# Block products in 13 of 16 half passes, sums in idle accumulator rows, early routing, and one chain for the last two passes

## The chip, the core and the metric

One core of a Trainium2 chip runs the whole program. The metric is device time in microseconds (us) of one execution, as a median of three timed runs: 757.85 us for the kernel before (757.56 to 758.64). Matrix products run on TensorE (PE, with PEld for its weight loads), elementwise work on VectorE (DVE), ScalarE (ACT) and GpSimd (POOL); SyncE (SP) issues nearly all transfers.

## The reference, cut to what matters

```
# 1. decayed linear attention, 2 x 8 heads, 768 tokens, head size 64  ->  x[1536, 512]
# 2. dense mixture, 4 experts, hidden 1024
for e in range(4):
    out += p[:, e:e+1] * (np.maximum(x @ w1[e], 0.0) @ w2[e])      # p: normalised domain_probs
# 3. mixture with one expert of 8 per token
logits = out @ w_gate;  expert_idx = argmax(logits);  gate_w = max(softmax(logits))
for e in range(8):
    mask = expert_idx == e
    y[mask] = gate_w[mask, None] * (np.maximum(out[mask] @ w1b[e], 0.0) @ w2b[e])
```

All in float32. The kernel writes each operand of a product as a high part (rounded to the fp32r type) and a low part (the remainder) and forms three products, high x high, low x high and high x low.

## The kernel before

**Passes.** Stage 2 is cut into 16 half passes `k` = 0 to 15. Passes 0 to 7 work on the first slab of 768 tokens, 8 to 15 on the second; `k % 8` names an expert and a half of its hidden units (512). A half pass multiplies `x` by a half of `w1` (the "h" products, with a relu and a split of the result) and then by a half of `w2` (the "y" products). Each y tile of 128 tokens is added into `acc[:, t, :]`, by DVE, or written there by ACT where `k % 8 == 0`.

**Plain and block passes.** A plain pass makes h with four row blocks and all tokens: 96 matmuls of 384 columns. A block pass (`fast_unit`, lines 567 to 631) splits `w1` and the tokens into 2 x 2 blocks and makes seven products in place of eight, as Strassen and Winograd do: 84 matmuls of 384 columns (`line` holds their order, product and half). It needs sums of weight blocks (`s1` to `s4`, made in `fast_steps`) and sums of token blocks (`t1` to `t4`), each as a high and a low part. Before, `FAST` holds 11 passes: 2 to 7 and 9 to 13. Passes 0, 1, 8, 14 and 15 are plain. During passes 1 and 8 (`plain_unit`) the token sums of the slab are made in small pieces (`tokens_steps`, lines 531 to 559), with scratch tiles of 384 columns.

**Kept weights.** The four tiles of weight blocks that a block pass of the first slab makes are stored to DRAM (`kept`) and fetched for the second slab's pass on the same expert half (`kept_steps`): passes 10 to 13 before.

**Attention** runs beside pass 0: `att_step` puts its matmuls between those of the pass, so many per unit as `paces` says. For the first slab its result goes straight into `xh` and `xl`, for the second into `x2`.

**Routing.** Each of 12 token tiles gets logits, a choice of expert (`route_choose`), a rank inside the expert and a scatter of its rows to DRAM rows `bins` (`route_send`). The logits of tiles 0 to 5 are made by DVE as row sums (`logit_v`, 8 per tile, one per expert, against rows of `wgt` in a ring of five buffers inside `x2`); those of tiles 6 to 11 by PE, with four transposes (`rtr`, `route_x`) and four small matmuls (`lg`). `bins` is first filled by one transfer (`open_routing`). Before, that fill and the routing of all tiles stand in passes 14 and 15, which run as three groups of 256 tokens, in each group pass 14 and then pass 15 (`moe1_group`).

**Order.** The program is recorded by hand in order (`manual_schedule`), and each engine runs its own instructions strictly in that order. `split_to(w, k, n)` makes the next `n` weight pieces as far as pass `k`; the hooks `hook1` (after each of 14 block products) and `hook2` (after each of 6 y tiles) place everything that isn't a matmul of the pass. PSUM gives three rotating banks `mm` to y tiles and plain h products, and four banks to the block products: product 1 of half `s` is copied by ACT to SBUF (`keep`, line 598) before products 6, 7 and 4 go on in its bank.

Of the kernel before, what the change touches and what calls it, by code (L numbers as in the profile page):

```python
# [40 lines left out]
FAST = [k for k in range(2, K1 - 2) if k != KS]  # L41
KEPT = [k for k in FAST if k >= KS and k - KS in FAST]
# [18 lines left out]
VT = TT  # L61
# [3 lines left out]
def body(ctx: ExitStack, tc: tile.TileContext, lam, att, dp, w1a, w2a, wg, wgt, w1b, w2b, out):  # L65
# [29 lines left out]
    lg_v = const.tile([P, TT, E2], F32, name="lg_v")  # L95
# [40 lines left out]
    def load_piece():  # L136
# [5 lines left out]
        if k < K1:  # L142
            src, e = (w1a, w2a)[w], k % KS // 2
        else:
            src, e = (w1b, w2b)[w], nth[(k - K1) // 2]
# [28 lines left out]
    def split_plain(n, c):  # L174
# [22 lines left out]
        k: dram.tile([len(PAIRS), P, 4, HF], F32, name=f"kept{k}") for k in FAST if k + KS in KEPT  # L197
# [7 lines left out]
    def fast_steps(n):  # L205
# [30 lines left out]
        def third():  # L236
            part("a22", raw(1, 1))
            add("s3", raw(0, 0), raw(0, 1), ALU.subtract)
            drop_raw()

        def fourth():
            add("s4", raw(1, 0), got["s2"], ALU.subtract, got["s2"])
            drop_raw()
            part("s1", got["s1"])

        return [
            sums,
            lambda: part("a11", raw(0, 0)),
            lambda: part("a12", raw(1, 0)),
            third,  # L250
            lambda: part("s2", got["s2"]),
            fourth,
            lambda: part("s3", got["s3"]),
            lambda: part("s4", got["s4"]),
        ]

    def kept_steps(n):
# [137 lines left out]
    def att_o(c):  # L395
# [29 lines left out]
        for r in range(2):  # L425
# [3 lines left out]
            else:  # L429
                hi_lo(xh[:, d, o:o + CH], xl[:, d, o:o + CH], xo[r], V)  # L430

# [63 lines left out]
    def moe1_mm2(k, hs, t0, j, midway=None, late="r"):  # L495
        t = t0 // P + j
        e = k % KS // 2
        ps = ps_mm.tile([P, 512], F32, tag="mm", name=f"y{k}_{t}")
        wh, wl = wt[1, k]
        parts = [((hh[:, j * P:j * P + P], hl[:, j * P:j * P + P]), (wh[:, f, :], wl[:, f, :]))  # L500
                 for f, (hh, hl) in enumerate(hs)]
        if midway:
            mm3(ps, parts[:FC // 2], True, False)
            midway()
            parts = parts[FC // 2:]
# [25 lines left out]
    def tokens_steps(g):  # L531
        def sums(d):
            f = {}

            def block(r, j):
                if g:
                    return x2[:, 2 * r + d, j * TH:j * TH + TH]
                return f[r, j]

            def whole():  # L540
                for i, (r, j) in enumerate([(0, 0), (0, 1), (1, 1), (1, 0)]):
                    f[r, j] = tmp(i, f"x{r}{j}_{d}")
                    a, b = (x[:, 2 * r + d, j * TH:j * TH + TH].bitcast(F32) for x in (xh, xl))
                    G.tensor_tensor(out=f[r, j], in0=a, in1=b, op=ALU.add)

            def one(n, i, a, b, op):
                t = f[n] = tmp(i, f"t{n}_{g}_{d}")
                V.tensor_tensor(out=t, in0=a(), in1=b(), op=op)  # L548
                hi, lo = st[f"t{n}"]
                hi_lo(hi[:, d, :], lo[:, d, :], t, V)  # L550

            return ([] if g else [whole, None]) + [
                lambda: one(1, 4, lambda: block(0, 1), lambda: block(0, 0), ALU.subtract),
                lambda: one(3, 5, lambda: block(1, 1), lambda: block(0, 1), ALU.subtract),
                lambda: one(2, 4, lambda: f[3], lambda: block(0, 0), ALU.add),
                lambda: one(4, 5, lambda: block(1, 0), lambda: f[2], ALU.subtract),
            ]

        return sums(0) + sums(1)

    def tokens_split(j):
        c = slice(j * TH, j * TH + TH)
        hi_lo(xh[:, :, c], xl[:, :, c], x2[:, :, c], V)


# [75 lines left out]
    def open_routing():  # L641
# [11 lines left out]
        for i in range(EN):  # L653
            G.memset(od["caps"][:, i:i + 1], float(BY_RANK[i]))
        rp = rt["rp"] = rt_ctx.enter_context(pool("rp", 2, side="right"))
        rt["ps_rt"] = rt_ctx.enter_context(pool("ps_rt", 2, space=PSUM))
        rt["ps_sm"] = rt_ctx.enter_context(pool("ps_sm", 3, space=PSUM))
# [5 lines left out]
        fill = rp.tile([P, W], F32, name="fill", bufs=1)  # L663
        G.memset(fill, 0.0)
        G.memset(fill.bitcast(I32)[:, DM + 1:W], FAR)
        SP.dma_start(
            out=bins.rearrange("(n p) w -> p n w", p=P),
            in_=fill.unsqueeze(1).to_broadcast([P, E2 * MOST // P, W]),
        )
# [29 lines left out]
    def route_choose(t, midway=None):  # L699
        rp = rt["rp"]  # L700
        if t < VT:
            lg = lg_v[:, t, :]
        else:
            xt = rt.pop((t, "xt"))
            lg = rt["ps_sm"].tile([P, P], F32, tag="sm", name=f"lg{t}")[:, :E2]
# [35 lines left out]
    def route_place(t):  # L741
        rp = rt["rp"]
# [4 lines left out]
        rank = rt["ps_sm"].tile([P, P], F32, tag="sm", name=f"rank{t}")[:, :E2]  # L747
# [20 lines left out]
    def route_row(t):  # L768
        gs = rt.pop((t, "gs"))
        pos = rt["rp"].tile([P, 1], I32, tag="pos", name=f"pos{t}", bufs=4)  # L770
# [55 lines left out]
    def route_order():  # L826
        count, place, places = od["count"], od["place"], od["places"]
        by_pair = od["tmp"][:, :EN * EN].rearrange("p (a b) -> p a b", a=EN)
        sm = rt["ps_sm"].tile([P, P], F32, tag="sm", name="counts")[:, :E2]
# [54 lines left out]
    def keep_up(n):  # L884
        warmup(rt["ps_sm"].tile([P, P], F32, tag="sm", name="warm_rt"), n)


    with tc.manual_schedule():
# [66 lines left out]
        def att_step():  # L955
# [8 lines left out]
            elif s == 1:  # L964
# [3 lines left out]
                if c == NC - 1:  # L968
                    at_ctx.close()
            else:  # L970
# [6 lines left out]

        rsteps = []
        rstage = (route_x, route_choose, lambda t: None, route_send)

        def route_step(t=None):

            for i, (t0, r) in enumerate(list(rsteps)):
                rstage[r](t0)
                rsteps[i] = (t0, r + 1)
            rsteps[:] = [x for x in rsteps if x[1] < len(rstage)]
            if t is not None:
                rsteps.append((t, 1 if t < VT else 0))

        paces = {0: (0, 1, 2, 2, 1, 0), 256: (1, 2, 2, 2, 1, 0), 512: (1, 2, 2, 2, 1, 0)}  # L990

        def moe1_group(k, t0, n, units, early=None):
            assert done["c"] >= (t0 + n) // CH - 1
            hs = []
            early = early or []

            def steps_of(i):
                for _ in range(paces[t0][i] if k == 0 and asteps else 0):
                    att_step()

            last = t0 + n == N
            for f in range(FC):
                hs.append(moe1_mm1(k, t0, n, f))
                steps_of(f)
                route_step(early.pop(0) if early else None)
                units(f)
            for j in range(n // P):
                t = t0 // P + j
                if t == NC - 1 and k == KL:
                    while rsteps:  # L1010
                        route_step()
                    first_load()
                    first_high(NC - 2)
                    split_to(0, k + 2, 2)
                    first_low(NC - 2)
                    moe1_mm2(k, hs, t0, j, lambda: route_x(NC - 2))
                    continue
                if last and k == KL:
                    split_to(0, k + 2, 2)
# [511 lines left out]
```

## Time and profile before

| | us |
|---|---|
| median of three timed runs | 757.85 |
| the profiled execution, its own time | 758.02 |
| span of its trace | 756.0 |
| pass 0 with attention (20.06 to 82.05) | 61.99 |
| pass 1, plain (82.05 to 116.88) | 34.83 |
| a block pass (148.45 to 179.99) | 31.54 |
| pass 8, plain (306.15 to 341.59) | 35.44 |
| passes 14 and 15, three groups | 24.11, 25.87, 27.41 |
| the rest, from 577.15 | 178.85 |

The profile shows one execution. An engine's busy time is read from its instructions; matmuls are pipelined, so a busy PE can still hide short stalls, and the time that a stretch takes is read from the starts in the chain of waits. That chain follows the work that ended last back to what released it.

### The profile page before, as it was taken

To read this page: it belongs to the slowest core of one execution; us is meant where nothing else is said; L and a number is where in the kernel's file an instruction comes from. 1 tells how busy PE (TensorE), PEld (TensorE's weight loads), DVE (VectorE), ACT (ScalarE), POOL (GpSimd) and SP (SyncE) were. 2 spreads that over 40 slices of the span, in tenths; PEclk is the share of its full clock that TensorE was granted. 3 is DMA by queue.
4 is the path that set the end of the run, shared out by engine and by line. 5 is a ranking of instruction groups with operands and counts; after the bars stand their busy time and mean duration, and the time that the engine had idled before them with its cause. 6 is when DMAs were issued, how large, how long until landed. Compare 5 with 4: busy or idle time off the path is not lost.

```text
span 756.0 us, 12472 instructions
## 1 busy us (share of the span) xinstructions
PE 740.2 (98%) x4736; PEld 667.5 (88%) x4736; DVE 494.4 (65%) x1079; ACT 309.6 (41%) x676; POOL 93.5 (12%) x98
## 2 busy tenths in 40 slices
PE   7999999999999999999999999999999999999995
PEld 7888889898898988889889898988898998998994
DVE  7444377676856767555377777777457867675883
ACT  4223335353343534345133141522124756665673
POOL 4563220000000000000000000003111013121013
PEclk9999999999999999999999999999999999999998
DMA  9774126627351122116171642286113877865660
GB/s 295 266 234 159 56 73 234 237 69 279 122 212 56 56 83 84 57 54 250 73 258 55 231 141 111 85 299 218 43 56 130 291 217 248 290 190 191 234 221 29
DMA packets 34314, 122.59 MB, mean 162 GB/s; under 512 B 4114, under 2 KB 6162, under 8 KB 31180
## 3 DMA queue, kind: packets, MB, share of 16 engines
q1 hardware_dynamic: 32139, 115.47, 44.6%
q0 software_dynamic: 2112, 6.31, 2.2%
q8 instruction: 38, 0.62, 0.3%
q14 instruction: 25, 0.20, 0.1%
HBM read 96.04 MB, written 25.92 MB: 161 GB/s over the span
## 4 chain that ended last, share of the span: by engine, by line
PE 73%; issue 17%; DVE 4%; POOL 2%; DMA 2%; ACT 1%; SPq 0%; POOLq 0%; ACTq 0%
PE y L469 35%; PE b L593 21%; PE h L469 9%; POOL out L112 2%; DMA att<-in_att 2%; PE qk L357 1%; PE xo L420 1%; PE xo L413 1%; PE z L1186 1%; DVE w1l L172 1%; PE lg L707 1%; PE u L441 0%; ACT w1h L171 0%; PE rtr L694 0%; DVE t L548 0%
## 5 line engine op out<-in xcount | busy, mean ns | idle before, releaser
L510 DVE SCALAR_TENSOR_TENSOR acc<-y,p_sb,acc 128x512 f32<-128x512 f32 x84 | 63.0, 750 | 65.3 <-PE y L469 62.1
L172 DVE TENSOR_TENSOR w1l<-raw,w1h 128x512 fp32r<-128x512 f32 x124 | 83.0, 692 | 16.6 <-ACT w1h L171 16.2
L171 ACT CAST w1h<-raw 128x512 fp32r<-128x512 f32 x128 | 75.3, 617 | 0.0
L600 ACT COPY u<-b 128x384 f32<-128x384 f32 x66 | 31.1, 475 | 100.2 <-PE b L593 98.9
L469 PE MATMUL h<-xh,w0h 128*128 128x256 f32 (+1 forms) x208 | 57.9, 308 | 1.0 <-ACT w0h L171 1.0
L172 DVE TENSOR_TENSOR w0l<-raw,w0h 128x512 fp32r<-128x512 f32 x80 | 52.5, 697 | 6.8 <-ACT w0h L171 6.3
L469 PE MATMUL h<-xh,w0l 128*128 128x256 f32 (+1 forms) x208 | 56.2, 298 | 0.0
L171 ACT CAST w0h<-raw 128x512 fp32r<-128x512 f32 x98 | 55.8, 619 | 0.3 <-DMA raw<-in_w1a 0.2
L593 PE MATMUL b<-xh,w0h 128*128 128x384 f32 x176 | 48.9, 338 | 0.0
L648 POOL IOTA places<- 128x7 f32 x1 | 0.2, 161 | 385.9 <-PE y L469 385.9
L112 POOL DMA_INDIRECT out<-y,xb x16 | 30.2, 1885 | 134.9 <-DVE y L1302 84.1
L469 PEld LDWEIGHTS h<-xh,w0h 128*128 128x128 f32 x208 | 38.2, 188 | 2.5 <-ACT w0h L171 1.2
L469 PEld LDWEIGHTS h<-xh,w0l 128*128 128x128 f32 x208 | 38.4, 189 | 0.4
L469 PE MATMUL g<-xg,w0h 128*128 128x288 f32 (+1 forms) x192 | 38.1, 293 | 0.0
L607 DVE TENSOR_TENSOR u<-b,u 128x384 f32<-128x384 f32 x66 | 36.4, 552 | 2.4 <-PE b L593 2.4
L469 PE MATMUL h<-xl,w0h 128*128 128x256 f32 (+1 forms) x208 | 37.0, 299 | 0.0
L684 DVE CUSTOM_DVE_ANT_0 x<-acc,x 128x512 f32<-128x512 f32 x48 | 32.9, 686 | 0.6
L593 PEld LDWEIGHTS b<-xh,w0h 128*128 128x128 f32 x176 | 32.3, 188 | 0.5
L469 PEld LDWEIGHTS h<-xl,w0h 128*128 128x128 f32 x208 | 31.2, 188 | 0.0
L469 PEld LDWEIGHTS g<-xg,w0h 128*128 128x128 f32 x192 | 30.8, 189 | 0.0
L593 PE MATMUL b<-xl,w0h 128*128 128x384 f32 x88 | 29.8, 339 | 0.0
L1186 PE MATMUL z<-g,w1h 128*128 128x352 f32 (+2 forms) x96 | 29.1, 366 | 0.8 <-DVE g L1208 0.7
(305 smaller groups left out, 2015.8 us busy)
## 6 DMA issues: line engine op xcount, KB each, us to landing
raw<-in_w2a SPq DMA_DIRECT2D x32, 512.0 KB, 3.6
raw<-in_w1b SPq DMA_DIRECT2D x32, 512.0 KB, 5.4
raw<-in_w2b SPq DMA_DIRECT2D x32, 512.0 KB, 4.9
att<-in_att SPq DMA_DIRECT2D x24, 512.0 KB, 5.1
raw<-in_w1a SPq DMA_DIRECT2D x22, 512.0 KB, 4.3
kept<-w0h SPq DMA_DIRECT2D x8, 1024.0 KB, 4.2
w0h<-kept SPq DMA_DIRECT2D x8, 1024.0 KB, 6.6
bins<-fill SPq DMA_DIRECT2D x1, 4626.0 KB
```

Of the source, the lines that this page charges most:

```text
L112: i = G.indirect_dma_start(out=dst, out_offset=bass.IndirectOffsetOnAxis(ap=idx, axis=0), in_=src, in_offset=None, bounds_check=rows - 1, ...
L171: A.copy(out=hi, in_=src)
L172: eng.tensor_tensor(out=lo, in0=src, in1=hi.bitcast(F32), op=ALU.subtract)
L357: T.matmul(qk[r][:, h, :], kT[64 * r:64 * r + 64, h, :], qT[64 * r:64 * r + 64, h, :], start=True, stop=True,)
L413: T.matmul(xo[r][o, h // 2, :], st[q, h, :], qd[q, h, :], start=h < 2, stop=False, skip_group_check=True,)
L469: T.matmul(ps, l, r, start=first and i == 0, stop=last and i == len(ops) - 1)
L510: V.scalar_tensor_tensor(out=acc[:, t, 0:DM], in0=ps, scalar=p_sb[:, t, e:e + 1], in1=acc[:, t, 0:DM], op0=ALU.mult, op1=ALU.add,)
L593: T.matmul(ps, l[:, d, c], r[:, d, :], start=first and i == 0, stop=i == len(ops) - 1, skip_group_check=not first,)
L600: A.copy(out=t, in_=bank[2, s])
L607: V.tensor_tensor(out=t, in0=bank[b, s], in1=t, op=ALU.add)
L684: V.tensor_tensor_reduce(out=x2.rearrange("p d t -> p (d t)")[:, RING * DM:], in0=acc[:, t, 0:DM], in1=logit_piece(e), scale=1.0, scalar=0 ...
L1186: T.matmul(ps[:, :2 * n], wh, both, start=i == 0, stop=False)
```

## The change

1. `FAST` takes in passes 1 and 8, so 13 passes are block passes. `half(k)` turns the order of the second slab's halves by two, so that passes 8 to 13 use the halves 2 to 7, all kept (six stores and fetches in place of four), and passes 14 and 15 use halves 0 and 1.
2. Token sums are made by DVE over both halves of the model dimension at once, in place, in `acc` rows 6 to 11, which hold nothing until pass 8: for the first slab during pass 0 (`x_acc` rows written by ACT or, for two tiles, by POOL), for the second during passes 2 to 5. The splits into `t1` to `t4` (`sum_split`) come at the end of pass 0 and in pass 7.
3. `bins` is filled in pass 1, by two transfers (512 columns of zeros, then 2 columns). Tiles 0 to 5 are chosen and sent in passes 12 and 13. Tiles 6, 7 and 8 get their logits from DVE in the last stage, each group of it now making all eight h products of both passes and then one chain of 24 matmuls per y tile.

```diff
-FAST = [k for k in range(2, K1 - 2) if k != KS]
-KEPT = [k for k in FAST if k >= KS and k - KS in FAST]
+FAST = range(1, K1 - 2)
+KEPT = range(KS, K1 - 2)
+def half(k):
+    return (k + k // KS * 2) % KS
-VT = TT
+VT = TT + 3
...
+        a11, a12, a22 = plain("a11", 0, 0), plain("a12", 1, 0), plain("a22", 1, 1)
+        s1, s2, s3, s4 = (summed(f"s{i}") for i in range(1, 5))
+        if k == 1:
+            return [a11, a12, a22, sums, s2, lambda: (third(), fourth()), s1, s3, s4]
...
+    def x_sum(n, g):
...
+        a, b, op, into = {
+            3: (x(1, 1), x(0, 1), ALU.subtract, (1, 1)),
+            1: (x(0, 1), x(0, 0), ALU.subtract, (0, 1)),
+            2: (x_acc(1, 1), x(0, 0), ALU.add, (0, 0)),
+            4: (x(1, 0), x_acc(0, 0), ALU.subtract, (1, 0)),
+        }[n]
+        V.tensor_tensor(out=x_acc(*into), in0=a, in1=b, op=op)
+    def sum_split(n):
+        src = x_acc(*{1: (0, 1), 2: (0, 0), 3: (1, 1), 4: (1, 0)}[n])
+        hi, lo = (t.rearrange("p d (c i) -> p c d i", c=3) for t in st[f"t{n}"])
+        hi_lo(hi, lo, src, V)
...
+    def fill_bins():
+        zeros = st["sf"].tile([P, 2, HF // 2], F32, tag="sf", name="zeros")
+        G.memset(zeros, 0.0)
...
+        for cols, src in ((slice(0, DM), zeros.rearrange("p a b -> p (a b)")),
+                          (slice(DM, W), rt["none"])):
+            SP.dma_start(
...
+                if t0 == 512 and i >= FC - 1:
+                    if i == FC - 1:
+                        split_to(0, 1, 2)
+                        sum_split(2)
+                    elif i == FC:
+                        split_to(0, 1, 2)
+                        sum_split(3)
+                        sum_split(1)
+                    else:
+                        split_to(0, 1, 2)
+                        sum_split(4)
...
+        k = K1 - 4
+        for t in range(4):
+            route_at(t, (k, 14 + t), (k, 16 + t))
+        for t in (4, 5):
+            route_at(t, (k + 1, 2 * t - 7), (k + 1, 2 * t - 3))
...
+            hs = []
+            for f in range(2 * FC):
+                hs.append(moe1_mm1(KL - 1 + f // FC, t0, 256, f % FC))
+                unit(f)
```

**DVE, from the last h of pass 0 on.** Before, pass 1 is plain and begins at once, with `w1l` its second weight and `x` the token blocks that POOL has to make first:

```order
L477 SCALAR_TENSOR_TENSOR ht_512_3l<-h_512_3_1064,ht_512_3h 128x256
L392 TENSOR_TENSOR a_0_1113<-qk_0_1101,dec 128x512
L392 TENSOR_TENSOR a_1_1114<-qk_1_1102,dec 128x512
L172 TENSOR_TENSOR w1l_994<-raw_386,w1h_993 128x512
L477 SCALAR_TENSOR_TENSOR ht_0_0l<-h_0_0_1192,ht_0_0h 128x384
L172 TENSOR_TENSOR w1l_994<-raw_485,w1h_993 128x512
L477 SCALAR_TENSOR_TENSOR ht_0_1l<-h_0_1_1221,ht_0_1h 128x384
L477 SCALAR_TENSOR_TENSOR ht_0_2l<-h_0_2_1238,ht_0_2h 128x384
L548 TENSOR_TENSOR t_0_0_1255<-x_0_1215,x_0_1213 128x384
```

Now twelve instructions (sums of weight blocks `s`, low parts of them in `w0h` and `w0l`, low parts of the token sums `t`) stand between pass 0 and the first instruction of block pass 1, `u`:

```order
L490 SCALAR_TENSOR_TENSOR ht_512_3l<-h_512_3_1106,ht_512_3h 128x256
L235 TENSOR_TENSOR s_1_1192<-raw_384,raw_386 128x512
L235 TENSOR_TENSOR s_1_1194<-s_1_1192,raw_384 128x512
L178 TENSOR_TENSOR w0l_1_909<-s_1_1194,w0l_1_909 128x512
L178 TENSOR_TENSOR t2l<-acc,t2h 128x3x2x128
L235 TENSOR_TENSOR s_1_1214<-raw_384 128x512
L235 TENSOR_TENSOR s_1_1194<-raw_386,s_1_1194 128x512
L178 TENSOR_TENSOR w0h_2_1221<-s_1_1192,w0h_2_1221 128x512
L178 TENSOR_TENSOR t3l<-acc,t3h 128x3x2x128
L178 TENSOR_TENSOR t1l<-acc,t1h 128x3x2x128
L178 TENSOR_TENSOR w0h_2_1221<-s_1_1214,w0h_2_1221 128x512
L178 TENSOR_TENSOR w0l_3_1244<-s_1_1194,w0l_3_1244 128x512
```

The work on sums moved from the inside of plain pass 1 to the seam in front of block pass 1.

**PE, the start of the second group of the last stage.** Before, the first h product (`h_1024_0`) is followed by a rank, the logits of a tile and the transposes of the next one:

```order
L469 MATMUL h_1024_0_5137<-xh,w0l_4604 128x256
L469 MATMUL h_1024_0_5137<-xl,w0h_4603 128x256 x4
L748 LDWEIGHTS upper
L748 MATMUL rank_5157<-oh_5088,upper 128x8
L750 LDWEIGHTS ones
L750 MATMUL rank_5157<-seen_5068,ones 128x8
L707 MATMUL lg_5173<-wg_sb,xt_5135 128x8 x4
L694 MATMUL rtr_5191<-ident,acc 128x128 x4
L469 MATMUL h_1024_1_5198<-xh,w0h_4603 128x256
```

Now one h product follows the other:

```order
L482 MATMUL y_7_5096<-w1l_4934,ht_768_3h 128x512
L482 MATMUL h_1024_0_5124<-xh,w0h_4790 128x256
L482 MATMUL h_1024_0_5124<-xh,w0l_4791 128x256
L482 MATMUL h_1024_0_5124<-xh,w0h_4790 128x256
L482 MATMUL h_1024_0_5124<-xh,w0l_4791 128x256
L482 MATMUL h_1024_0_5124<-xh,w0h_4790 128x256
L482 MATMUL h_1024_0_5124<-xh,w0l_4791 128x256
L482 MATMUL h_1024_0_5124<-xh,w0h_4790 128x256
L482 MATMUL h_1024_0_5124<-xh,w0l_4791 128x256
L482 MATMUL h_1024_0_5124<-xl,w0h_4790 128x256 x4
L482 MATMUL h_1024_1_5142<-xh,w0h_4790 128x256
```

The transposes, the logits and the rank that stood between the two products are gone from this place.

**SP, around the fill of `bins`.** Before, it stands between the weights of pass 15 (`in_w2a`) and those of stage 3 (`in_w1b`):

```order
L156 DMA raw_4629<-in_w1a 128x1024
L156 DMA raw_4651<-in_w2a 128x1024
L156 DMA raw_4671<-in_w2a 128x1024
L666 DMA bins<-fill 128x18x514
L156 DMA raw_4791<-in_w1b 128x1024
L156 DMA raw_4862<-in_w1b 128x1024
```

Now it stands, in two parts, between the first and the second weights of pass 2:

```order
L162 DMA raw_1216<-in_w1a 128x1024
L162 DMA raw_1219<-in_w1a 128x1024
L680 DMA bins<-zeros 128x18x512
L680 DMA bins<-none 128x18x2
L162 DMA raw_1289<-in_w2a 128x1024
L162 DMA raw_1330<-in_w2a 128x1024
```

The fill moved past twelve passes of weight traffic, and its last two columns became a transfer of their own.

## Rows read from the trace of the kernel before

**Rows 1.** The page, part 1: busy us, share of the span, instructions.

```profile
PE 740.2 (98%) x4736; PEld 667.5 (88%) x4736; DVE 494.4 (65%) x1079; ACT 309.6 (41%) x676; POOL 93.5 (12%) x98
```

**Rows 2.** Chain of waits, passes 1 and 2: start us, us, what.

```profile
82.05 8.48 PE h L469 x48
...
103.30 0.50 ACT ht_1h L476
...
116.88 14.71 PE b L593 x84
```

**Rows 3.** Windows: us, busy us of PE, PEld, DVE, ACT, POOL, clock, DMA share, GB/s.

```profile
20.06:82.05 61.99, 61.99 (x774) 52.98 (x774) 26.84 (x53) 17.96 (x41) 29.46 (x30) 1.00 0.60 203
82.05:116.88 34.83, 34.34 (x170) 30.43 (x169) 22.74 (x39) 12.93 (x26) 10.52 (x9) 1.00 0.26 94
148.45:179.99 31.54, 31.54 (x157) 28.24 (x157) 21.30 (x35) 12.59 (x25) 0.00 (x0) 1.00 0.49 185
306.15:341.59 35.44, 34.07 (x169) 30.47 (x169) 21.83 (x39) 15.83 (x31) 0.00 (x0) 1.00 0.22 66
436.45:468.09 31.64, 31.64 (x157) 28.19 (x157) 23.89 (x54) 8.49 (x18) 0.00 (x0) 1.00 0.40 150
499.76:523.87 24.11, 23.45 (x154) 20.65 (x154) 19.67 (x90) 8.44 (x26) 4.50 (x4) 1.00 0.98 322
523.87:549.74 25.87, 25.87 (x179) 23.49 (x177) 11.67 (x54) 4.81 (x16) 3.89 (x4) 1.00 0.11 42
549.74:577.15 27.41, 27.35 (x193) 24.73 (x190) 16.41 (x51) 9.88 (x25) 2.15 (x2) 1.00 0.31 94
```

**Rows 4.** Chain of waits in the last stage.

```profile
517.96 0.17 PE rank L748
...
523.92 0.49 PE rtr L694 x4
...
525.89 0.90 PE lg L707 x8
...
532.67 5.72 PE y L469 x24
538.39 5.75 PE h L469 x48
```

**Rows 5.** Groups by line and shape: count | busy us, mean ns | idle before, releaser.

```profile
L172 DVE TENSOR_TENSOR w1l<-raw,w1h 128x512 fp32r<-128x512 f32 x124 | 83.0, 692 | 16.6 <-ACT w1h L171 16.2
L171 ACT CAST w1h<-raw 128x512 fp32r<-128x512 f32 x128 | 75.3, 617 | 0.0
...
L684 DVE CUSTOM_DVE_ANT_0 x<-acc,x 128x512 f32<-128x512 f32 x48 | 32.9, 686 | 0.6
...
L600 ACT COPY u<-b 128x384 f32<-128x384 f32 x66 | 31.1, 475 | 100.2 <-PE b L593 98.9
...
L508 ACT ACTIVATE acc<-y,p_sb 128x512 f32<-128x512 f32 x12 | 8.3, 689 | 27.0 <-PE y L469 23.0 <-DVE p_sb L944 3.9
```

**Rows 6.** Instructions on tile x: ns min/median/max, first and last start.

```profile
L171 ACT CAST xh<-x x2: 1476/1476/1477, 291.9 to 294.4; 128x1536 fp32r<-128x1536 f32 x2
L172 DVE TENSOR_TENSOR xl<-x,xh x2: 1749/1751/1753, 294.0 to 297.5; 128x1536 fp32r<-128x1536 f32 x2
```

**Rows 7.** Instructions on bins: ns min/median/max, first and last start us.

```profile
L112 POOL DMA_INDIRECT bins<-acc,pos x12: 972/974/1334, 515.4 to 583.8; - x12
...
L666 SPq DMA_DIRECT2D bins<-fill x1: 402/402/402, 496.6 to 496.6; - x1
```

**Rows 8.** The page, parts 2, 3 and 6: packets; queues; us to landing.

```profile
DMA packets 34314, 122.59 MB, mean 162 GB/s; under 512 B 4114, under 2 KB 6162, under 8 KB 31180
...
q1 hardware_dynamic: 32139, 115.47, 44.6%
q0 software_dynamic: 2112, 6.31, 2.2%
...
raw<-in_w2a SPq DMA_DIRECT2D x32, 512.0 KB, 3.6
```

More of the change, by code (lines that the diff above doesn't have):

```diff
@@ L196, in body @@
     kept = {
-        k: dram.tile([len(PAIRS), P, 4, HF], F32, name=f"kept{k}") for k in FAST if k + KS in KEPT
+        k: dram.tile([len(PAIRS), P, 4, HF], F32, name=f"kept{k}") for k in map(half, KEPT)
     }
@@ L430, in att_o @@
                 hi_lo(xh[:, d, o:o + CH], xl[:, d, o:o + CH], xo[r], V)
+                if c >= B:
+                    A.copy(
+                        out=acc[:, TT + c, 2 * r * P:2 * r * P + 2 * P].rearrange(
+                            "p (d i) -> p d i", d=2),
+                        in_=xo[r],
+                    )
     def att_u(c):
@@ L526, in tmp @@
         return st["fx"].tile([P, TH], F32, tag=f"c{i}", name=name)
[L531 to L559, printed above, removed]
@@ L662, in open_routing, with small @@
         )
[L663 to L669, printed above, removed]
+    def small(name):
+        rt["sm"].append(rt["sm"].pop(0))
+        return rt["sm"][-1].tile([P, P], F32, tag="sm", name=name)
     RING = 5
@@ L746, in route_place @@
         A.activation(out=ex, in_=df, func=AF.Exp, accum_out=gs)
-        rank = rt["ps_sm"].tile([P, P], F32, tag="sm", name=f"rank{t}")[:, :E2]
+        rank = small(f"rank{t}")[:, :E2]
         T.matmul(rank, upper, oh, start=True, stop=prev is None)
@@ L884, in keep_up @@
     def keep_up(n):
-        warmup(rt["ps_sm"].tile([P, P], F32, tag="sm", name="warm_rt"), n)
+        warmup(small("warm_rt"), n)
     with tc.manual_schedule():
@@ L992, in moe1_group @@
[L992 to L998, printed above, removed]
-                    att_step()
[L1001 to L1019, printed above, removed]
-                moe1_mm2(k, hs, t0, j)
-                steps_of(FC + j)
-                route_step(
-                    t if k == KL and t < NC - 2 else early.pop(0) if early else None
-                )
-                units(FC + j)
@@ L1056, in body @@
-        logits = []
-        for k in range(1, K1 - 2):
-            if k not in FAST:
-                plain_unit(k)
-                if k == KS:
-                    for e in range(RING):
-                        logit_load(e)
-                    logits = [(t, e) for e in range(E2) for t in range(TT)]
-                continue
+                elif t0 == 256:
+                    if i % 2:
+                        split_to(0, 1)
+                    if i < B:
+                        x_whole(i)
+                    elif i >= FC:
+                        x_sum((3, 1)[i - FC], 0)
+                elif i < 2:
+                    x_sum((2, 4)[i], 0)
@@ new lines, in body, with at, route_at @@
+            for f in range(FC):
+                hs.append(moe1_mm1(0, t0, 256, f))
+                unit(f)
+            for j in range(256 // P):
+                moe1_mm2(0, hs, t0, j)
+                unit(FC + j)
+        plan = {}
+        def at(hook, what, *args):
+            plan.setdefault(hook, []).append(lambda: what(*args))
+        def route_at(t, choose, send):
+            at(choose, route_choose, t)
+            at(send, route_send, t)
+        k = K1 - 4
+        for t in range(4):
+            route_at(t, (k, 14 + t), (k, 16 + t))
@@ L1081, in hook2 @@
                 if k in KEPT:
-                    logit(2)
+                    logit(2 if k == KS else 2 - j % 2)
+                for step in plan.pop((k, 14 + j), []):
+                    step()
             fast_unit(k, hook1, hook2)
             split_to(0, k + 1, 8)
+            if k == KS - 1:
+                for e in range(RING):
+                    logit_load(e)
+                logits = [(t, e) for e in range(E2) for t in range(TT)]
         assert not logits
         st_ctx.close()
-        open_routing()
```

192 lines of the change are left out of this document (118 added, 74 removed).

## The prediction

> **What bounds the kernel now.** I read the page's first part, then the chain of waits, then a table of windows cut at the passes, then groups of instructions by shape. TensorE is busy 740.2 us, 98% of the span [rows 1], at a granted clock of 1.00 in every stretch read [rows 3]. So the time goes down if matmuls go or if one of the few gaps goes, and up where another engine makes a new gap. DVE is busy 65% and ACT 41% [rows 1]; they matter by when they deliver, not by how much they do.
>
> The chain gives the price of a matmul. In the plain pass 48 h products of 384 columns take 8.48 us, .177 each; a block pass takes 14.71 us for its 84, .175 each, and 16.85 us for 72 y products [rows 2]. The sum 14.7 + 16.85 is the 31.54 of a whole block pass, in which PE is never idle [rows 3]. The two plain passes to be changed take 34.83 and 35.44 us [rows 3]; in the first the chain leaves PE from 103.30 to 109.82 for ACT, DVE and the token sums [rows 2]. In the last stage PE alone is the chain but for logits, transposes and a rank [rows 4].
>
> The sum goes against the profiled run's own time, 758.02 us (span 756.0 and 2.0 around it), .2 above the median of the three runs, 757.85. T is the end of pass 0 on PE, 82.05 in the run before.
>
> **Pass 1: -3.1 us.** 96 h products become 84: 34.83 - 31.54 = 3.29 us if PE never waits [rows 3]; 96 x .177 - 84 x .175 = 2.3 of it is work, 1 us the stalls. What is new is the seam: the block operands must be ready when pass 0 ends. Attention's last DVE work lies before the last two y tiles of pass 0 (2 x 2.8 us), so I let DVE begin at T-5.7 on the twelve instructions that the order shows: eight of 128x512 at .692 [rows 5], four splits of 128x768, which the trace does not have. Between .69 at 512 elements and 1.75 at 1536 [rows 5, 6] I interpolate .96. That is 5.5 + 3.8 = 9.4 us, T+3.7 at the end. ACT has the matching casts (.617 at 512, 1.476 at 1536 [rows 5, 6], .83 at 768), two evacuations of y at .689, and then the `keep` copy of .475 [rows 5]. The last evacuation can't start before T; behind it two casts, a cast of 768 and the copy are .69 + 1.23 + .83 + .48 = 3.2, so it ends at T+3.3 (a little overlap counted). PE wants that bank after three products of 6 matmuls, 18 x .175 = T+3.15. I take a wait of .2 us. The low parts are wanted by products at T+6.3 and T+10.5, when they are done. Ends of the range: no wait at all, or, if ACT and DVE wait for one another at every step, 9.4 + 5.8 us in series from T-5.7, T+9.5, the copy at T+9.9 and a wait of 6.8 us. I take the value near the lower end because the casts don't read what DVE writes except for the four sums. The sums themselves move into pass 0, where DVE is busy 26.8 of 62.0 us and POOL 29.5 [rows 3], and are priced at nothing; if DVE were full there they would add 4 x .96.
>
> **Pass 8: -3.9 us.** 35.44 - 31.54 [rows 3]. Its seam has more room: the splits come in pass 7's y stage, where DVE has six updates at .75 and eight instructions at .96, 12.2 of 16.85 us, ACT eight casts at .83, 6.6. The four raw sums lie in passes 2 to 5, where DVE is busy 21.3 of 31.5 us [rows 3]; one more at .96 is covered. Its four weight tiles are fetched and not made. If that cover went, one 128x768 pair too late would cost .96 + .83.
>
> **Last stage: -5.2 us.** An h of 48 matmuls and 256 columns takes 5.75 us, two y tiles' half 5.72 [rows 4]; a group of four such stretches is 2 x 5.75 + 2 x 5.72 = 22.94.
> Group 1: 24.11 before, PE busy 23.45 with DVE at 19.67 [rows 3]; the rank at 517.96 [rows 4] stands behind a crowded DVE that routes early tiles. These tiles leave: 24.11 - 22.94 = -1.17.
> Group 2: 25.87 before [rows 3] with transposes (.49) and logits (about .90) of two tiles [rows 4]. These go and a rank of .17 stays: 22.94 + .17 - 25.87 = -2.76.
> Group 3: 27.41 before [rows 3]; one of its tiles loses transposes and logits, about -1.3. Tiles 9 to 11 and the tail behind the last y stay, and so does the rest, 178.85 us.
> DVE pays 24 row sums of .686 [rows 5], 16.5 us over three groups, and sheds six tiles' routing and half of the `acc` updates. Its worst place is one tile's eight sums and an update, 5.5 + .75, against a y stretch of 5.72; I see it hidden since nothing on PE waits for a logit within that stretch.
>
> **Early routing: +0.5 us.** Six tiles' ranks, .17 each, come to stand between the products of passes 12 and 13. Such a pass is at 31.64 us with DVE at 23.9 [rows 3]. Ends: nothing (they may fill bubbles) and 6 x .17 = 1.0; I take the middle.
>
> **The fill: 0 in the sum.** Before, it is issued at 496.6 and the first scatter, which needs it, starts at 515.4 [rows 7]: it landed within 18.8 us. Now POOL must first clear the zeros, so it starts near T+6 and lands near T+25. DVE needs the zeros' buffer for a sum of pass 2 at T+20 and stands until T+25; PE would feel it when its sixth y tile wants a bank, T+14.7 + 5 x 2.81 = T+28.75, some 2.3 us later than DVE has caught up. The weights of pass 2 behind the fill are wanted near T+33 and land in 3.6 us [rows 8]. Ends: nothing, or the slower rival below.
>
> What speaks about the strip of two columns, 2304 pieces of 8 bytes, in the trace: of 4114 packets under 512 B, q0 can hold 2112 at most [rows 8], so some 1900 or more lie on other queues; I read most of these as the 8-byte tails of the old fill's 2056-byte rows, and that fill landed in 18.8 us all the same. A rule speaks against the strip: the Trainium skill, "DMA: Bandwidth & Descriptors", section Specifications, says that a transfer under 512 B is done as a read-modify-write and doesn't reach line rate. The trace agrees that such packets were there and doesn't show them slow; the page gives no price, and by it the sum would move toward rival (c).
>
> **Sum.** -3.1 - 3.9 - 1.17 - 2.76 - 1.3 + .5 = -11.7 us; 758.02 - 11.7 = 746.3.
>
> **Rivals.**
> (a) The seam isn't hidden: ACT and DVE alternate and PE stands up to 6.8 us in pass 1. For it: ACT's casts wait for y's evacuation, and DVE's four low sums depend on ACT. Against: most steps are independent. It gives up to 746.3 - .2 + 6.8 = 752.9; half of that wait gives 749.5.
> (b) DVE binds in the last stage: each of three tiles is late by 5.49 + .75 - 5.72 = .52, with the ranks late behind it, in all 1.6 us: 747.9. For it: DVE at 19.67 of 24.11 in group 1 [rows 3]. Against: in group 2, DVE at 11.67 plus one tile's 5.5, less updates, leaves a quarter free.
> (c) Slower: the strip holds the queue. Taken by packets, 44.6% of 16 x 756 us over 32139 packets is .168 us each [rows 8]; 2304/16 = 144 per engine are 24.2 us. The next weights then land at T + 25 + 24.2 + 3.6, near T+52.7; ACT, in order, stands at their cast from T+33 with two casts (1.2) before the copy due at T+35.7. PE loses 18.2 us: 764.5, and every pass behind is late by it. It decides against the change once the strip holds the queue 18 us. For it: that price. Against: the old fill, whose tails were as small.
> (d) The block form doesn't pay in passes 1 and 8, because PE's gaps only move: -11.7 + 7.0 leaves 753.3.
>
> **How the numbers follow.** Main case 71%, between 743.5 (group 1's and 3's gaps wider than thought, no waits) and 748.5. (a) 13%, (b) 8%, (c) 5%, (d) 3%. The range 743.5 to 752.5 holds the main case, (b) and most of (a); what is left out is (c), (d) and the tail of (a). The change can be told from none at about .2%, 1.5 us; only (c) is slower, with a little for something unseen: 6%. No difference needs two rivals at once: 2%. Faster 92%.
>
> **What would show it.** In the chain after: pass 1 as 84 b products of 14.7 us and 72 y products of 16.85 from about 82, with a gap of PE of no more than .2 us where the second half's product 6 takes a bank at T+3.15 (a gap of several us there is (a)). Pass 8 at 31.5. Groups of the last stage at about 22.9, 23.1 and 26.1, PE the releaser throughout (DVE naming the gaps is (b)). In pass 1's y tiles DVE waits for the fill, PE does not. Weights of pass 2 that land after T+36, and ACT waiting for them, is (c). The forecast is wrong in its main term if PE is idle over 1 us in either seam, and right by accident if passes 1 and 8 give less than 6 us and the last stage more than 7.

## The result, and the profile after

The changed kernel takes 748.69 us, the median of four runs (748.51 to 749.54); the ratio to the kernel before is .988, 95% interval .9863 to .9897. That is 9.1 us faster where 11.7 were forecast, inside the range and .2 above the 748.5 that ended the main case. Its profiled execution took 748.51 us with a span of 746.7.

Part 1 of the page, against [rows 1]:

```profile
PE 732.0 (98%) x4676; PEld 660.6 (88%) x4676; DVE 505.1 (68%) x1113; ACT 310.8 (42%) x679; POOL 85.0 (11%) x91
```

TensorE has 60 matmuls and 8.2 us less, DVE has 10.7 us more. PE is as full as before.

The windows of the changed kernel, cut where PE starts a stretch, answer [rows 3]. Columns are as there. In order: passes 1, 3, 8, 12, 13, then groups 1 and 2 of the last stage and the h products of group 3.

```profile
81.31:113.01 31.70, 31.70 (x157) 28.34 (x156) 23.42 (x38) 14.88 (x30) 3.19 (x3) 1.00 0.86 265
144.72:176.42 31.70, 31.70 (x157) 28.40 (x156) 22.09 (x36) 12.48 (x25) 0.00 (x0) 1.00 0.50 185
303.25:334.96 31.71, 31.71 (x158) 28.40 (x157) 19.94 (x44) 12.07 (x23) 0.00 (x0) 1.00 0.58 208
430.04:462.23 32.19, 32.19 (x164) 28.16 (x163) 21.58 (x75) 9.85 (x26) 2.96 (x3) 1.00 0.44 164
462.23:495.36 33.13, 32.20 (x163) 28.53 (x163) 24.44 (x69) 15.23 (x34) 3.55 (x5) 1.00 0.38 128
495.36:518.10 22.74, 22.74 (x146) 20.55 (x144) 11.62 (x24) 5.10 (x12) 0.00 (x0) 1.00 0.32 93
518.10:540.99 22.89, 22.89 (x147) 20.52 (x146) 16.16 (x54) 3.37 (x10) 0.01 (x1) 1.00 0.16 51
540.99:554.94 13.95, 13.41 (x116) 13.19 (x114) 12.98 (x63) 5.99 (x18) 2.92 (x3) 1.00 0.29 96
```

Passes 1 and 8 went from 34.83 and 35.44 us to 31.70 and 31.71 [rows 3]. But pass 3, whose matmuls the change leaves alone (DVE gets one sum more), went from 31.54 to 31.70 as well, with PE busy throughout. And pass 13 takes 33.13 us with 32.20 of PE, where such a pass took 31.64 [rows 3].

All differences of the two traces, from the starts of PE's products in the timelines, sum to the 9.4 us by which the first `g` product of stage 3 starts earlier:

| stretch | before | after | forecast | measured |
|---|---|---|---|---|
| to the end of pass 0 | 81.89 | 81.31 | 0 | -.6 |
| pass 1 | 34.83 | 31.70 | -3.1 | -3.1 |
| passes 2 to 7 | 189.27 | 190.24 | 0 | +1.0 |
| pass 8 | 35.44 | 31.71 | -3.9 | -3.7 |
| passes 9 to 11 | 94.86 | 95.08 | 0 | +.2 |
| passes 12 and 13 | 63.31 | 65.32 | +.5 | +2.0 |
| group 1 | 24.18 | 22.74 | -1.2 | -1.4 |
| group 2 | 25.80 | 22.89 | -2.8 | -2.9 |
| group 3 to the first `g` | 33.66 | 32.86 | -1.3 | -.8 |

(The chain of [rows 2 to 4] puts its starts some .15 us later than the timeline, so single rows differ by that.) What was forecast to be gained was gained: -12.0 for -12.2 in passes 1 and 8 and the last stage. What the forecast doesn't have took 2.7 us back: 1.2 in passes whose matmuls stayed, and 1.5 more than allowed for in passes 12 and 13.

PE's waits in the changed kernel, by engine and line waited for, show the second (us in total, times, longest):

```profile
PE rank L776 <- DVE rk_all L783: 0.9, 1, 0.9
PE rank L776 <- DVE oh L748: 0.5, 1, 0.5
```

The first stands in pass 13, the second in group 3. The timeline around the first (start us, us, engine, line, instruction; in brackets the idle time before it and its releaser):

```profile
468.67 0.18 PE L776 MATMUL rank<-oh,upper 128*128 128x8 bf16 x1
...
469.58 0.68 DVE L178 TENSOR_TENSOR w1l<-raw,w1h 128x512 fp32r<-128x512 f32 x1
470.18 0.55 DVE L620 TENSOR_TENSOR u<-b,u 128x384 f32<-128x384 f32 x1
470.76 0.52 ACT L489 ACTIVATE ht_001h<-u 128x384 fp32r<-128x384 f32 x1 [1.61 <-DVE u L620]
...
471.32 0.56 DVE L490 SCALAR_TENSOR_TENSOR ht_001l<-u,ht_001h 128x384 fp32r<-128x384 f32 x1 [0.59 <-ACT ht_001h L489]
...
471.80 0.16 DVE L783 CUSTOM_DVE_ANT_0 jk<-rank,oh 128x8 f32<-128x8 f32 x1
...
472.02 0.17 PE L776 MATMUL rank<-oh,upper 128*128 128x8 bf16 x1 [0.93 <-DVE rk_all L783]
```

The rank of tile 4 is on PE at 468.7. DVE reads it (`jk`) only at 471.80, behind the choice of tile 5, a weight split, a sum and a hidden tile's low part. Until then the one PSUM bank for ranks is taken, and the rank of tile 5 holds PE's queue.

### The profile page after: what moved, and what is told of

Its sections match the earlier page's. It is cut to its first block, busy times and chain, and to the rows that moved or that the text cites. A ratio compares the mean times of both kernels' runs of the same rounds, so it can differ in the third digit from the quotient of the medians.

```text
span 746.7 us, 12406 instructions
## 1 busy us (share of the span) xinstructions
PE 732.0 (98%) x4676; PEld 660.6 (88%) x4676; DVE 505.1 (68%) x1113; ACT 310.8 (42%) x679; POOL 85.0 (11%) x91
## 5 line engine op out<-in xcount | busy, mean ns | idle before, releaser
L118 POOL DMA_INDIRECT bins<-acc,pos x12 | 12.6, 1048 | 468.4 <-DVE mx L742 376.3
L606 PE MATMUL b<-xh,w0h 128*128 128x384 f32 x208 | 57.7, 338 | 0.0
L712 DVE CUSTOM_DVE_ANT_0 x<-acc,x 128x512 f32<-128x512 f32 x72 | 49.4, 686 | 1.0
L620 DVE TENSOR_TENSOR u<-b,u 128x384 f32<-128x384 f32 x78 | 43.0, 552 | 1.8 <-PE b L606 1.8
L482 PE MATMUL h<-xh,w0h 128*128 128x256 f32 x144 | 35.8, 292 | 1.0 <-ACT w0h L177 1.0
L482 PE MATMUL h<-xh,w0l 128*128 128x256 f32 x144 | 34.5, 280 | 0.0
L606 PE MATMUL b<-t1h,w0h 128*128 128x384 f32 x104 | 31.0, 339 | 0.0
L606 PE MATMUL b<-t3h,w0h 128*128 128x384 f32 x104 | 29.1, 339 | 0.0
L606 PE MATMUL b<-t4h,w0l 128*128 128x384 f32 x104 | 28.9, 338 | 0.0
L606 PE MATMUL b<-t2h,w0l 128*128 128x384 f32 x104 | 28.9, 338 | 0.0
```

What stands on the lines that cost most here:

```text
L118: i = G.indirect_dma_start(out=dst, out_offset=bass.IndirectOffsetOnAxis(ap=idx, axis=0), in_=src, in_offset=None, bounds_check=rows - 1, ...
L482: T.matmul(ps, l, r, start=first and i == 0, stop=last and i == len(ops) - 1)
L606: T.matmul(ps, l[:, d, c], r[:, d, :], start=first and i == 0, stop=i == len(ops) - 1, skip_group_check=not first,)
L620: V.tensor_tensor(out=t, in0=bank[b, s], in1=t, op=ALU.add)
L712: V.tensor_tensor_reduce(out=x2.rearrange("p d t -> p (d t)")[:, RING * DM:], in0=acc[:, t, 0:DM], in1=logit_piece(e), scale=1.0, scalar=0 ...
```

## Experiments

Three numbers are compared: the median, the stretch in question, and the stretch from PE's end of pass 0 to its first `g` product ("the core stretch"), which leaves out the differences at the start of a run; it is 492.54 us in the first profile of the changed kernel (501.35 before) and 492.61 in the second. Its last part, from the logits behind the last y tile to that `g` product, takes 7.24 us in both, but 7.24 to 7.73 in the profiles of the variants (and 9.87 in one, of which the last section tells), so a difference of less than half a microsecond between two core stretches shows nothing.

**1. The tiles of the token sums moved.** In the built programs the kernel before has its weights and token sums at an odd multiple of 32 bytes and `x` at an even one; the changed kernel has weights at an even one and sums and `x` at an odd one, because `lg_v`, which lies below weights and `x`, holds the logits of three more tiles, 96 bytes. (The sums moved by 1600 bytes, which leaves them at an odd multiple.) The pad stands ahead of the sums on their side of the memory and moves them by 32 bytes, and with them the scratch of the weight sums, the tiles `u` and the small tiles of the routing.

```diff
             od[name] = op.tile([P, n], d, name=name)
+        od["pad"] = op.tile([P, 8], F32, name="pad")
+        G.memset(od["pad"], 0.0)
```

> The tiles of the token sums move by 32 bytes (a pad of 8 floats); nothing else changes. In the kernel before, weights and token sums both lay at an odd multiple of 32 bytes and the 48 products on token sums went at .173 us each, those on x, which lay at an even multiple, at .177; in the changed kernel the weights lie at an even and the rest at an odd multiple, and all 84 go at .177 (14.84 us a pass for 14.69). Theory 'same place': a product goes faster when both its operands lie at the same offset modulo 64 bytes. Then 48 x .0035 = .15 us a pass come back, b stretches at 14.69 again, 13 x .15 = 2.0 us faster, about 746.7. Rival 'crowding': the changed kernel's DVE and transfers beside the products slow them: b stretches stay at 14.84 and the time at 748.7.

Measured: 747.39 us (746.93 to 750.02; ratio .9871, .9854 to .9888), a core stretch of 490.93. A window over the block products of pass 2, of the changed kernel:

```profile
113.01:127.85 14.84, 14.84 (x86) 14.84 (x84) 9.96 (x17) 7.75 (x17) 0.00 (x0) 1.00 0.72 286
```

and of this kernel:

```profile
113.41:128.09 14.68, 14.68 (x86) 14.68 (x85) 9.81 (x17) 7.77 (x17) 0.00 (x0) 1.00 0.73 284
```

The DMA share and ACT's work are the same, DVE's is .15 us less; PE takes .16 us less. "Crowding" falls. From the differences of consecutive starts over four passes, a product on token sums takes 176.7 ns in the changed kernel and 173.3 here; one on `x` takes 176.7 and 176.5. The core stretch is 1.6 us less, and 1.85 without its last part, which takes 7.48 us here.

**2. The operands beside the weights moved.** The pad above, and one behind `acc`, which moves `x`, the hidden tiles and stage 3's tiles:

```diff
     acc = accp.tile([P, NC, W], F32, name="acc")
+    gap = accp.tile([P, 8], F32, name="gap")
+    G.memset(gap, 0.0)
```

> Tokens, hidden tiles and token sums all move by 32 bytes, so that they lie at the same offset modulo 64 bytes as the weights. 'Same place': all 84 products of a block pass at .173, 14.55 us, another 36 x .0035 x 13 = 1.6 us beyond the run with the sums alone; y products, now .234 each, gain a similar .003 at 72 a pass, up to 13 x .25 = 3.3 us, and products of stage 3 as well: 738 to 745. 'Crowding': no change, 748.7.

Measured: 745.49 us (744.70 to 747.03; ratio .9837, .9824 to .9851), a core stretch of 489.66. Windows over the block and the y products of pass 2:

```profile
113.12:127.76 14.64, 14.64 (x86) 14.64 (x84) 9.81 (x17) 7.75 (x17) 0.00 (x0) 1.00 0.75 296
127.76:144.56 16.80, 16.80 (x74) 13.52 (x74) 12.13 (x19) 4.72 (x9) 0.00 (x0) 1.00 0.53 192
```

A further gain, just short of what was expected: `x` products 175.5 ns and not 173, y 16.80 us for 16.87. "Same place" was too simple.

**3. The kernel before with its token sums moved.** A pad behind the `t` tiles of `open_fast`.

```diff
                 fx.tile([P, 2, TH], F32R, name=f"t{i}{x}") for x in "hl"
             )
+        gap = fx.tile([P, 8], F32, name="gap")
+        G.memset(gap, 0.0)
```

> The kernel before, with its tiles of token sums moved by 32 bytes, so that they lie at an even multiple and the weights at an odd one; nothing else changes. 'Same place': block stretches go from 14.69 to 14.84, 11 x .15 = 1.65 us slower, 759.5. 'Addresses matter in another way' (the same tiles at an even multiple were the faster ones in the changed kernel): 757.9 or less.

Measured: 758.25 us (757.82 to 759.56; ratio 1.0004, .9994 to 1.0013), no change. A window over the block products of pass 3:

```profile
147.93:162.60 14.67, 14.67 (x85) 14.67 (x84) 9.18 (x16) 7.86 (x17) 0.00 (x0) 1.00 0.46 175
```

It stays at 14.67, where "same place" asked for 14.84 (the kernel before has 14.69 here). That theory falls: sums and weights at unlike offsets are slow in the changed kernel and not here.

**4. Only the tiles that PE reads.** The same three lines in the changed kernel: `t` moves, the tiles `u` of ACT and DVE stay.

> Of the tiles beside the products, those of the token sums that PE reads (and the scratch of weight sums) move by 32 bytes; the tiles that ACT copies a product into and DVE adds to stay. Theory 'where PE reads': the products on token sums go from .1767 to .173 us as when all of these moved, a block stretch 14.67. Rival 'where ACT and DVE write': they stay at .1767 and the stretch at 14.84.

Measured: 746.97 us (746.65 to 750.32; ratio .9871, .9855 to .9888), against 749.14 (748.87 to 749.41) for the changed kernel in the same set; a core stretch of 490.71.

```profile
112.70:127.38 14.68, 14.68 (x86) 14.67 (x84) 9.82 (x17) 7.77 (x17) 0.00 (x0) 1.00 0.73 288
```

The place where PE reads decides: 1.9 us of the core stretch. The scratch of the weight sums moved along, but pass 8 makes no weight sums, and nothing touches that scratch during its block products; they too go back, from the first row (the changed kernel) to the second (this one):

```profile
303.25:318.09 14.84, 14.84 (x86) 14.84 (x84) 10.05 (x17) 7.85 (x17) 0.00 (x0) 1.00 0.65 215
301.87:316.54 14.67, 14.67 (x86) 14.67 (x84) 10.04 (x17) 7.87 (x17) 0.00 (x0) 1.00 0.65 213
```

**5. One send two products later.**

```diff
-            route_at(t, (k + 1, 2 * t - 7), (k + 1, 2 * t - 3))
+            route_at(t, (k + 1, 2 * t - 7), (k + 1, 4 * t - 11))
```

> Tile 5 is sent after block product 10 of pass 13 in place of product 8; nothing else changes. Theory 'one bank': early routing has one PSUM bank for ranks, and the rank of tile 5 stands on PE until DVE has read the rank of tile 4 (.93 us idle, 1.17 with what lies around it). Two products later the read is over: 1.0 to 1.2 us faster, about 747.6. Rival 'crowded DVE': DVE reaches the reads late wherever they stand, since sums, splits and low parts of weights fill it in block products: PE stands as long at the new place, 748.7.

Measured: 748.64 us (748.19 to 749.42; ratio .9881, .9865 to .9896), a core stretch of 492.51: nothing. PE's timeline in pass 13, with ACT's:

```profile
474.15 0.52 ACT L489 ACTIVATE ht_110h<-u 128x384 fp32r<-128x384 f32 x1 [1.58 <-DVE u L620]
474.58 0.46 ACT L613 COPY u<-b 128x384 f32<-128x384 f32 x1
...
475.10 0.44 PE L606 MATMUL b<-t4h,w0l 128*128 128x384 f32 x1 [0.47 <-ACT u L613]
```

The wait of .93 us at the rank is gone, and one of .47 stands behind it: PE waits for ACT's copy, ACT for a sum on DVE, which is late. The bank was where it showed, not why. The block stretch got .35 us shorter (15.93 for 16.28), and the last part of the core stretch was .28 longer (7.52 us), within what that part differs from profile to profile.

**6. Tiles 4 and 5 beside the y products.**

```diff
-            route_at(t, (k + 1, 2 * t - 7), (k + 1, 2 * t - 3))
+            route_at(t, (k + 1, 10 + t), (k + 1, 12 + t))
```

> Tiles 4 and 5 are chosen and sent beside the y products of pass 13, in place of its block products; nothing else changes. Moving one send by two products gained nothing: the wait at the rank went, and PE stood .47 us for a copy by ACT, which stood for sums by DVE. Theory 'crowded DVE': the block products' own sums and splits leave DVE no room for 14 instructions a tile; in the y stage there is room (12 of 16.85 us). Then the block stretch of pass 13 goes back from 16.28 to 14.85 us, its y stretch grows by .25 as that of pass 12 did with four tiles (.48): 1.2 us faster, 747.5. Rival 'ranks cost PE wherever they stand': the y stretch grows by what the block stretch loses: 748.7.

Measured: 748.58 us, of 747.95 to 751.57 (ratio .9870, .9855 to .9886), with the odd profile of which the last section tells: inconclusive. So it was run once more, beside the changed kernel itself:

> The changed kernel unaltered, as a measure for the next two runs of this set: 748.7. In profiled runs of its variants pass 0 ends on PE between 81.31 and 82.54 us, so its start differs by about 1 us from run to run; this profile shows whether the 81.31 us of the first one was an early case (then up to 82.5) or the rule.

Measured: 749.14 us (748.87 to 749.41; ratio .9886, .9871 to .9901); pass 0 ended at 82.22, .9 later than in its first profile.

> Tiles 4 and 5 routed beside the y products of pass 13, once more, since the first set had three usable times (747.95 to 748.59) and a profile in which PE's granted clock fell to .50 for 6.8 us after a wait for the first routed rows. Theory 'crowded DVE': with the clock at 1.00 in the routing, the PE stretch from the end of pass 0 to the first g product is 1.0 to 1.5 us shorter than the changed kernel's 492.54, and the time 747.2 to 747.7. Rival 'given back later': the stretch ends at 492.5 and the time is 748.6.

Measured: 748.08 us (747.70 to 751.77; ratio .9886, .9868 to .9905), a core stretch of 491.69. The changed kernel's windows over the block and y products of pass 13, from the second profile:

```profile
463.17:479.44 16.27, 15.34 (x92) 14.96 (x91) 12.64 (x50) 7.75 (x20) 3.24 (x4) 1.00 0.38 130
479.44:496.31 16.87, 16.87 (x74) 13.56 (x73) 11.81 (x20) 7.50 (x14) 0.30 (x1) 1.00 0.38 126
```

and those of this kernel:

```profile
462.28:477.20 14.92, 14.92 (x88) 14.92 (x87) 10.01 (x23) 7.89 (x17) 1.13 (x2) 1.00 0.31 107
477.20:494.35 17.15, 17.15 (x77) 13.49 (x77) 14.58 (x46) 7.71 (x18) 2.27 (x3) 1.00 0.44 147
```

1.35 us less and .28 more: 1.07 gained, and most of it kept: the core stretch is .92 less, the median 1.06. The medians alone would not carry this (in the first set 748.58 stood against 748.69), the windows do. "Crowded DVE" named the right engine and half of the reason: DVE is busier beside the y products (14.58 of 17.15 us) than it was beside the block products (12.64 of 16.27). What the y products lack is the chain from PE through DVE and ACT back to PE that the rows of experiment 5 show; this part of the reason is read from the rows and was not tested by itself.

**7. Logits of tiles 6 to 8 on PE again.**

```diff
-VT = TT + 3
+VT = TT
...
-                at(8 + i, logit_v, *x)
...
+        at(16, route_x, a)
         route_at(a, 17, 18)
+        at(18, route_x, b)
         route_at(b, 19, 21)
...
+        at(22, route_x, c)
```

> Tiles 6, 7 and 8 get their logits from PE again (four transposes and a set of small products each), DVE's 24 row sums go; the rest stays. My terms: .35 to .49 and .8 to .9 us per tile on PE, three tiles, 3.5 to 4.2 us slower, 752.2 to 752.9. Rival 'DVE binds there': what DVE gains takes back part of it, 1.6 us or more: 750 to 751.3.

Measured: 751.37 us (751.15 to 754.17; ratio .9927, .9913 to .9940), which looks like the rival. The windows over the last stage say otherwise, of the changed kernel:

```profile
495.36:573.85 78.49, 77.72 (x537) 70.38 (x535) 51.80 (x183) 20.56 (x57) 5.19 (x5) 1.00 0.30 93
```

and of this one:

```profile
494.22:576.34 82.12, 81.70 (x572) 74.25 (x570) 37.06 (x135) 22.22 (x60) 5.18 (x5) 1.00 0.22 69
```

3.63 us more in the stage, inside my 3.5 to 4.2 (3.27 without its last part, 7.60 us for 7.24, still more than the rival left); DVE sheds 14.7 us there and gives PE .35 us of idle time back at most (.77 to .42). Most of the rest was returned elsewhere: the smaller `lg_v` moves weights, `x` and hidden tiles back by 96 bytes, and block stretches take 14.73 us for 14.84.

**8. The kernel before with the new order of attention.**

```diff
-        paces = {0: (0, 1, 2, 2, 1, 0), 256: (1, 2, 2, 2, 1, 0), 512: (1, 2, 2, 2, 1, 0)}
+        paces = {0: (0, 1, 2, 2, 1, 0), 256: (1, 2, 2, 2, 2, 0), 512: (2, 2, 2, 1, 0, 0)}
```

> The kernel before, with the changed kernel's distribution of attention steps over the units of pass 0, alone. In the changed kernel pass 0 ends on PE at 81.31 us, in the one before at 81.9 to 82.05, though its h products start .27 later. Theory 'order': fewer changes between attention and products, .6 to .7 us faster, 757.2. Rival 'other cause' (sums by DVE in pass 0, addresses, the first transfers): 757.9 as before.

Measured: 757.92 us (757.46 to 758.21; ratio .9998, .9989 to 1.0007): nothing. With the end of pass 0 between 81.17 and 82.54 us in the profiles of the changed kernel and its variants, the -.6 of the table lies within what runs differ by.

**9. The version that the runs point to**: the pads of experiment 2 and the edit of experiment 6.

> The changed kernel with all moved by 32 bytes (measured alone at 745.5) and with tiles 4 and 5 routed beside the y products of pass 13. If both reasons hold they add: 745.5 - 1.2 = 744.3. If routing's place is worth nothing: 745.5.

Measured: 743.81 us (743.52 to 746.48; ratio to the kernel before .9818, .9802 to .9834), a core stretch of 488.12: 1.54 us less than with the pads alone, or 1.14 without its last part (7.33 us for 7.73), where experiment 6 gained 1.07. The two reasons add, and this kernel is 14 us faster than the first and 4.9 faster than the changed one.

## Why the prediction was right, and where its sum was off

The sum was 2.7 us too good, and the measured time lies inside the range only because the range reached beyond the main case for rivals (a) and (b), which did not come. The large terms hold by their mechanism; two of their numbers fit in part by luck, as said below.

**Pass 1 and its seam: right in mechanism.** The hand-over ran almost as it was worked out. DVE's rows at the seam of the changed kernel:

```profile
77.91 0.69 DVE L178 TENSOR_TENSOR w0l<-s,w0l 128x512 fp32r<-128x512 f32 x1 [0.73 <-ACT w0l L177]
...
81.33 0.95 DVE L178 TENSOR_TENSOR t3l<-acc,t3h 128x768 fp32r<-128x768 f32 x1
...
84.27 0.95 DVE L178 TENSOR_TENSOR t4l<-acc,t4h 128x768 fp32r<-128x768 f32 x1
85.14 0.55 DVE L620 TENSOR_TENSOR u<-b,u 128x384 f32<-128x384 f32 x1
```

The split of 768 columns takes .95 us for .96 interpolated, and DVE is through its twelve instructions at T+3.8 for T+3.7 (T is 81.31 here). That fit is partly luck: the splits follow one another at .87 us, start to start, and most of the others at .60, faster than the .96 and .69 that were added up, and a wait of .73 us for ACT's cast (first row) fills the difference. ACT's copy and the product that waits for it:

```profile
83.86 0.48 ACT L613 COPY u<-b 128x384 f32<-128x384 f32 x1
```

```profile
84.48 0.36 PE L606 MATMUL b<-t2h,w0l 128*128 128x384 f32 x1
```

The copy ends at T+3.03, the product starts at T+3.17: no wait shows, where .2 was allowed for. Rival (a) didn't come, with .14 us to spare, and rival (d) neither. The pass gave 3.13 us for 3.1 because two misses cancel: the wait of .2 that stayed away, and .16 of slower products, of which more below.

**Pass 8** gave 3.73 for 3.9; the rest is the slower products.

**The last stage** gave 5.2 us for 5.2, again with misses that cancel. Groups 1 and 2 gave .27 and .15 more than forecast. Group 3 gave .8 for 1.3, and not all of it where it was forecast. The starts of the logits behind its last y tile, before and after:

```profile
575.64 0.98 PE L707 MATMUL lg<-wg_sb,xt 128*128 128x8 f32 x8
566.61 0.95 PE L735 MATMUL lg<-wg_sb,xt 128*128 128x8 f32 x8
```

From the group's first matmul to there it took 26.06 us before and 25.62 now, .44 less; the other .36 lies behind, in the part that was to stay as it is. In the group a rank waits .54 us for DVE's choice. That wait is the one trace of rival (b), and experiment 7 measures the trade: 3.6 us of PE against 14.7 of DVE, which hid but for at most .35.

**The fill: nothing, as forecast, but by another path.** SP's rows (the transfer queue's issues) in the changed kernel:

```profile
86.87 0.41 SPq L680 DMA_DIRECT2D bins<-zeros  x1
87.31 3.12 SPq L680 DMA_DIRECT2D bins<-none  x1
90.48 12.68 SPq L162 DMA_DIRECT2D raw<-in_w2a  x2
```

The page gives 16.5 us from the issue of the zeros to their landing, so they landed at 103.4 (T+22, where T+25 was forecast). The sum of pass 2 that reuses their buffer is DVE's third:

```profile
103.83 0.68 DVE L235 TENSOR_TENSOR s<-raw 128x512 f32<-128x512 f32 x1
```

It stands .4 us behind the landing, and DVE did not wait for it (the instruction before starts at 103.23, and such instructions follow one another at .60 us), so the standstill of DVE that the prediction saw, from T+20 to T+25, did not come. The two weights behind the strip hold SP until 103.2; the first of them landed 18.9 us after its issue (3.8 is the median of such weights), at 109.4 or T+28. So fill and strip did hold the queue, but ACT's cast of this weight comes 5 us later, at 114.7, and no PE wait stands in passes 1 to 3: rival (c) didn't come.

Its price was wrong too. The packets in a window over the old fill, before, and over the strip, now:

```profile
DMA packets 2745, 6.32 MB, mean 324 GB/s; under 512 B 58, under 2 KB 58, under 8 KB 2744
DMA packets 2432, 0.23 MB, mean 85 GB/s; under 512 B 2336, under 2 KB 2336, under 8 KB 2431
```

The first (496.5 to 516 us) holds no 2304 small packets: the rows of 2056 bytes went out whole, and the packets under 512 B that the prediction read as their tails [rows 8] are others. So the argument "against" rival (c) had no ground. The second (99.9 to 102.6) holds the 2304 pieces of the strip, done in 2.7 us where (c) took 24.2, at .168 us a packet.

**Where the sum failed, first: "a whole block pass is 31.54".** I carried a duration from one program to another. The same 84 products took 14.84 us in place of 14.69 because the tiles had moved: .16 us in each of passes 2 to 7, 1.0 us in the table, and the same share of passes 1 and 8. Another place for the sums gives 1.6 and 1.9 us of core stretch (experiments 1 and 4).

**Second: "early routing, I take the middle", +.5.** The term counted PE's ranks and took DVE's room from an average over the pass, 23.9 of 31.64 [rows 3]. In the block stretch of pass 13 the routing raises DVE to 12.64 us of 16.27 (10.01 of 14.92 without it), in short instructions that stand in line ahead of sums which ACT, then PE, wait for. It cost 2.0 us in place of .5, of which about 1.1 goes when those tiles move to the y products (experiment 6); of the rest .5 stands in the y products of pass 12, with the ranks of four tiles between them (17.35 us for 16.87), and .28 stays as the cost of the other two tiles in the y products of pass 13. The range's upper bound for this term, 1.0, was too low: it bounded what PE does and not what DVE makes it wait.

## What to carry to other kernels

Look at what the new work stands in front of, and not only at an engine's busy share: DVE had room left in the block stretch and more work in the y stretch, and yet the routing cost PE 1.35 us in the one and .28 in the other. Small instructions ahead of a chain that leads back to PE delay PE. When a wait goes and no time is won, look for the next wait behind it before blaming the resource that showed it. Where untouched stretches change their pace with every engine's work the same, look at what an edit did to the addresses of the tiles.

## What the runs showed of the hardware

- **A product's time depends on where its operands lie.** A 384-column matmul on token sums took 176.7 ns or 173.3 by a move of the sums by 32 bytes (experiments 1 and 4), and 174.7 where weights and `x` had moved by 96 bytes and the sums had not (experiment 7). What the rule is stays open. Like offsets modulo 64 bytes were the first guess, and experiment 3 speaks against it. Offsets modulo 64 are not the whole rule: in experiment 3 sums and `x` both lie at an even multiple of 32 bytes and the weights at an odd one, and a product takes 173.5 ns on sums and 176.5 on `x`.
- **The granted clock can fall in the routing.** Seven runs of the variants were 1.5 to 3.7 us longer than the median of their kernel's runs (746.48, 747.03, 750.02, 750.32, 751.57, 751.77, 754.17). Their mean granted clock is .991 to .994, that of all other runs of these kernels .996 to .998, so in each of them the clock stood lower for a part of the time. One of them, of the kernel of experiment 6, has a profile; its windows from 566 us on:

```profile
566.00:572.00 6.00, 5.12 (x61) 4.74 (x59) 3.87 (x19) 1.40 (x4) 0.00 (x0) 0.99 0.42 119
572.00:576.30 4.30, 4.28 (x24) 4.13 (x23) 2.37 (x18) 1.22 (x5) 1.94 (x2) 0.50 0.16 61
576.30:586.20 9.90, 9.90 (x67) 9.90 (x65) 9.18 (x28) 7.61 (x22) 0.00 (x0) 0.88 0.68 192
```

The clock (third column from the end) is at .50, 1.2 GHz, in the second window and for part of the third. Before, PE had waited .81 us for the first routed rows (a wait that the changed kernel's first profile doesn't have) and was busy 5.12 of 6.00 us. Its first 64 `g` products took 9.95 us where the changed kernel took 8.81. In this profile the wait stands ahead of the fall; that it caused it, and that the other six runs lost their clock at the same place, is likely and not shown.
